# Value products in concurrent 64x64 and 32-row tiles of the TensorE array, with V loaded by head halves in rows of 64

## The chip, the cores and the metric

The kernel runs on one core of one Trainium2 chip. The metric is the device time of one execution in microseconds (us). Each kernel was run several times, in rounds that alternate with the kernel before on the same chip. Every comparison below is between fast runs. Only one timed run of any kernel here was slow, and it is left out.

## The reference, cut to what matters

```python
# q, k, v: (8 batches, 8 heads, 576 positions, 64), float32
k_p = k.reshape(B, H, 72, 8, 64).mean(axis=3)        # keys pooled by 8: 72 a head
v_p = v.reshape(B, H, 72, 8, 64).mean(axis=3)        # values pooled by 8
scores = matmul(q, k_p.T) / sqrt(64)
attn = exp(scores - max); attn = attn / sum(attn)
x = (attn @ v_p), heads side by side                 # (8 * 576 tokens, 512)
out = gelu(x @ w_in) @ w_out                         # 512 -> 2048 -> 512
```

## The kernel before

Attention of one batch is woven into the two big products of the batch before it ("hidden", L296, and "output", L301). Seven batches of 512 positions are handled this way in a steady rhythm. Batch 0 stands in the start, and the last 64 positions of every batch form a "rest" batch. The parts that the change touches:

```python
    def rows(t, b):                                   # pooled rows: 72 a head, 576 a batch, each of 8 x 64 numbers
        return t[b].rearrange("h (sp pl) d -> (h sp) pl d", pl=8)

    def load_half(b, which, eng):                     # 64 rows of k and 64 of v share one block of 128 partitions
        if which == "v":
            eng.dma_start(out=st[b]["kv"][64:128, 4], in_=rows(v, b)[0:64])
        else:
            eng.dma_start(out=st[b]["kv"][0:64, 4], in_=rows(k, b)[512:576])

    def load_main(b, which, c0, c1, eng):             # the other 512 rows, on 128 partitions
        t, w0, b0 = (k, 0, 0) if which == "k" else (v, 64, 5)
        src = rows(t, b)[w0 + 128 * c0:w0 + 128 * c1].rearrange("(c p) pl d -> p c pl d", p=128)
        eng.dma_start(out=st[b]["kv"][:, b0 + c0:b0 + c1], in_=src)
    ...
    def values(g, half, eng):                         # "value step": pooled v (masked, zero-padded) times e
            ...
                for x, (c, n) in enumerate(PARTS[pr]):
                    nc.tensor.matmul(out=xo[:, i, :], lhsT=vbd[:, g, n, :], rhs=eT[:, :, c, :],
                                     start=(x == 0), stop=(x == 1))
    ...
    def load_kv(n):                                   # all on one queue, in this order
            ...
            load_main(b, "k", 0, 4, nc.sync)
            load_half(b, "k", nc.sync)
            load_half(b, "v", nc.sync)
            load_main(b, "v", 0, 4, nc.sync)
    ...
                at(hooks, t0, pool, b, 0, 5)          # hooks: position among the matmuls of a batch
                at(hooks, t0, k_transpose_dma, b)     # kvb -> kTd, a DMA on the same queue as the loads
                at(hooks, t0 + 20, pool, b, 5, 9)     # v is pooled later than k
                at(hooks, 56, k_spread, b, ...)       # kTd -> kbd; the scores (from hook 67) wait for it
                ...
            at(hooks, 91, load_kv, n2)
```

In the views, DVE pools `kv` into `kvb`, `kTd<-kvb` is the DMA transpose of the pooled k, and `kbd` is its copy that the scores `sc` multiply. `eb` holds the normalised exponentials, `eT<-eb` are their DMA transposes, `xo` is the result of the value step, and `xT` is its copy for the hidden layer. Line numbers differ from kernel to kernel, so follow the tile names.

The softmax here doesn't subtract the row's maximum and nothing guards it: scores larger than these inputs give would overflow.

## Time and profile before

| | kernel before |
|---|---|
| time, median | 301.14 us (300.99 to 301.49, 4 runs) |
| span of the profiled run, granted TensorE clock | 299.3 us, 1.00 |
| first value step of the steady rhythm | 52.14 us |
| from one steady value step to the next | 30.35 us |
| value step, start of the last matmul before to the start of the first after | 1.94 us |
| k landed, v landed, kTd landed after a value step (batch at 142.77) | 6.9, 10.9, 14.6 us |
| scores begin after a value step | 17.70 us |

In the view of DMA issues each line gives tile, queue, kind, count, size, and the median time from issue to landing. These lines are of the kernel before:

```profile
kv<-in_v_dram SPq DMA_DIRECT2D x7, 1024.0 KB, 9.9
...
eT<-eb SPq DMA_TRANSPOSE x32, 2.6
...
kTd<-kvb SPq DMA_TRANSPOSE x6, 3.6
```

The lines that carry the bound (busy shares, chain) stand in the prediction. kTd lands 14.6 to 16.3 us after a value step, and the scores that need it start at 17.70. So PE's slack there is only 1.4 to 3.1 us, and the two copies into kbd take 0.5 to 1.1 us of it. And kTd is issued at 10.8 to 12.8 us, in the same queue as v, when v has just landed or is still on its way.

### The profile page before, as it was taken

The page shows a single profiled execution, that of the slowest core. Times are in us where ns is not written, and L with a number is a line of the kernel's source. Part 1 is how long each engine was busy: PE and PEld are TensorE (multiplying, and loading weights), DVE is VectorE, ACT ScalarE, POOL GpSimd, SP SyncE. Part 2 cuts the span into 40 slices and gives each one's busy share as a digit, 9 for nine tenths or more (in the row PEclk, how much of TensorE's full clock was granted, in tenths as well). Part 3 has the DMA queues.
Part 4 walks back from the last instruction along what each step waited for, and adds up shares of the span by engine and source line. Part 5 has one row for each costly group of instructions (what it writes and reads, how often), then busy time and mean ns, then how long its engine had stood idle before and what let it go on. Part 6 is the DMA issues. An engine that isn't in the chain of part 4 may idle for free.

```text
span 299.3 us, 4581 instructions
## 1 busy us (share of the span) xinstructions
PE 290.7 (97%) x1734; PEld 151.6 (51%) x1734; DVE 146.7 (49%) x241; ACT 158.2 (53%) x242; POOL 55.5 (19%) x71
## 2 busy tenths in 40 slices
PE   7869999999999999999999999999999999999996
PEld 7748844445444544454445444544444544444444
DVE  6895769164706570648073807381639100920012
ACT  1477783667157715672477246724773267426500
POOL 3252033230400240024012400240024000100000
PEclk9999999999999999999999999999999999999999
DMA  7999997995699459947993599049944800351012
GB/s 235 357 387 338 384 350 132 343 279 158 135 279 250 145 127 271 269 146 126 261 297 134 119 249 301 4 107 249 276 147 101 164 36 2 79 114 37 0 70 70
DMA packets 73221, 56.32 MB, mean 188 GB/s; under 512 B 45808, under 2 KB 55408, under 8 KB 73200
## 3 DMA queue, kind: packets, MB, share of 16 engines
q1 hardware_dynamic: 73056, 55.98, 68.2%
q8 instruction: 13, 0.21, 0.3%
q10 hardware_dynamic: 144, 0.07, 0.1%
q14 instruction: 8, 0.07, 0.1%
HBM read 36.70 MB, written 9.44 MB: 154 GB/s over the span
## 4 chain that ended last, share of the span: by engine, by line
PE 91%; DMA 3%; DVE 2%; SPq 1%; POOL 1%; issue 0%; POOLq 0%
PE mm L296 41%; PE mm L301 41%; PE xo L266 4%; DMA q_sb<-in_q_dram 3%; PE sc L208 2%; PE mm L329 1%; POOL eb L231 1%; SPq L98 1%; PE xo L272 1%; PE tp L193 1%; PE sc L213 0%; DVE w_in_b L80 0%; PE tp L240 0%; DVE w_out_b L80 0%; POOL q_b L80 0%; PE xo L255 0%
## 5 line engine op out<-in xcount | busy, mean ns | idle before, releaser
L301 PE MATMUL mm<-w_out_b,gT 128*128 128x512 bf16 x560 | 128.6, 379 | 0.5 <-DVE w_out_b L80 0.5
L296 PE MATMUL mm<-xT,w_in_b 128*128 128x512 bf16 (+1 forms) x640 | 127.6, 358 | 0.5 <-DVE xT L80 0.5
L298 ACT ACTIVATE gT<-mm 128x512 bf16<-128x512 f32 (+1 forms) x160 | 88.4, 555 | 47.0 <-PE mm L296 45.9
L296 PEld LDWEIGHTS <-w_in_b 128*128 128x128 bf16 x640 | 62.2, 98 | 62.6 <-issue 0.5
L301 PEld LDWEIGHTS <-gT 128*128 128x128 bf16 x560 | 53.4, 98 | 59.7 <-DVE w_out_b L80 0.7
L80 DVE COPY osb<-mm 128x512 f32<-128x512 f32 (+2 forms) x37 | 24.3, 658 | 62.9 <-PE mm L301 60.8
L78 ACT CAST xT<-xo 128x1024 bf16<-128x1024 f32 (+1 forms) x18 | 16.6, 966 | 56.8 <-PE xo L266 49.1
L228 DVE TENSOR_REDUCE den<-e 128x8 f32<-128x576 f32 x36 | 26.5, 736 | 38.0 <-ACT e L221 37.9
L148 POOL TENSOR_TENSOR vbd<-kvb,vmask 128x256 bf16<-128x256 bf16 (+2 forms) x40 | 21.2, 553 | 113.5 <-DVE kvb L130 113.4
L128 DVE TENSOR_TENSOR kv<-kv 128x1024 f32<-128x1024 f32 (+3 forms) x20 | 22.4, 1118 | 29.7 <-DMA kv<-in_v_dram 27.7
L231 DVE TENSOR_TENSOR eb<-e,r 128x576 bf16<-128x576 f32 x28 | 27.2, 970 | 1.0
L221 ACT ACTIVATE e<-sc 128x576 f32<-128x576 f32 x36 | 22.5, 650 | 9.6 <-ACT e L221 4.0
L231 POOL TENSOR_TENSOR eb<-e,r 128x576 bf16<-128x576 f32 x8 | 10.1, 1266 | 71.5 <-ACT e L221 41.1
L80 POOL CAST q_b<-q_sb 128x2048 bf16<-128x2048 f32 (+1 forms) x7 | 15.0, 2147 | 4.1 <-DMA q_sb<-in_q_dram 4.1
L208 PEld LDWEIGHTS <-qT 128*128 128x128 bf16 x128 | 10.1, 98 | 7.0 <-ACT qT L78 0.6
L208 PE MATMUL sc<-kbd,qT 128*128 128x144 bf16 x128 | 13.2, 226 | 0.2 <-ACT qT L78 0.2
L266 PE MATMUL xo<-eT,vbd 128*128 128x512 bf16 x56 | 13.2, 379 | 0.0
L129 DVE TENSOR_TENSOR kv<-kv 128x512 f32<-128x512 f32 (+3 forms) x20 | 12.8, 640 | 0.7
L410 PE MATMUL warm<-identb 128*128 128x128 bf16 x112 | 9.1, 249 | 1.4 <-POOL vmask L398 1.4
L494 ACT ACT_TABLE_LOAD x8 | 10.3, 1283 | 0.1
L80 DVE COPY kbd<-kTd 64x288 bf16<-64x288 bf16 x12 | 5.6, 467 | 8.3 <-DMA kTd<-kvb 8.2
L314 ACT ACT_TABLE_LOAD x7 | 9.0, 1283 | 0.1
(55 smaller groups left out, 99.5 us busy)
## 6 DMA issues: line engine op xcount, KB each, us to landing
out_dram<-osb SPq DMA_DIRECT2D x31, 256.0 KB, 6.7
kv<-in_k_dram SPq DMA_DIRECT2D x7, 1024.0 KB, 6.5
q_sb<-in_q_dram SPq DMA_DIRECT2D x7, 1024.0 KB, 5.9
kv<-in_v_dram SPq DMA_DIRECT2D x7, 1024.0 KB, 9.9
w_in_s<-in_moe_w_in_dram SPq DMA_DIRECT2D x4, 1024.0 KB, 13.0
w_out_s<-in_moe_w_out_dram SPq DMA_DIRECT2D x4, 1024.0 KB, 13.8
out_dram<-osb SPq DMA_DIRECT2D x9, 128.0 KB, 2.3
kv<-in_k_dram SPq DMA_DIRECT2D x2, 512.0 KB, 3.9
```

Of the source, the lines that this page charges most:

```text
L78: eng.copy(out=out, in_=in_)
L80: eng.tensor_copy(out=out, in_=in_)
L128: add(out=t[:, :, 0:4, :], in0=t[:, :, 0:4, :], in1=t[:, :, 4:8, :], op=ALU.add)
L148: eng.tensor_tensor(out=vbd[p0:128, b, n0:n1, :].rearrange("p (c r) (hh d) -> p c (r hh) d", c=max(m, 1), d=D), in0=kvb[p0:128, 4 + c0:4 + ...
L208: nc.tensor.matmul(out=o, lhsT=qT[:, j, pr, :], rhs=kbd[:, g, pr].rearrange("d hh s -> d (hh s)"), start=True, stop=True)
L221: nc.scalar.activation(out=e.rearrange("p (x h) s -> p x (h s)", x=2), in_=sc[:, :, 0:4 * Sp], func=ACT.Exp, scale=1.0 / 64.0)
L228: nc.vector.reduce_sum(out=den, in_=e, axis=AX.X)
L231: eng.tensor_tensor(out=eb[:, j, 128 * 5 - W:].rearrange("p (h s) -> p h s", s=Sp), in0=e, in1=r.unsqueeze(2).to_broadcast([128, H, Sp]), ...
L266: nc.tensor.matmul(out=xo[:, i, :], lhsT=vbd[:, g, n, :], rhs=eT[:, :, c, :], start=(x == 0), stop=(x == 1))
L296: nc.tensor.matmul(out=hp[:, 0:c1 - c0], lhsT=w_in_b[:, ko, fo * 128:(fo + 1) * 128], rhs=st[g]["xT"][:, ko, c0:c1], start=(ko == 0), stop ...
L298: nc.scalar.activation(out=gT[:, fo, c0:c1], in_=hp[:, 0:c1 - c0], func=ACT.Gelu_apprx_tanh)
L301: nc.tensor.matmul(out=o, lhsT=gT[:, fo, r * 128:(r + 1) * 128], rhs=w_out_b[:, fo, :], start=(fo == 0), stop=(fo == FO - 1))
```

## The change

The value product used 128x128 weights padded with zeros, because a head's 72 pooled rows don't fill whole partitions. The change stores v so that 64 rows of a head fill 64 neighbouring partitions. Heads 0 to 3 lie in the lower half, heads 4 to 7 in the upper. The remaining 8 rows of every head are gathered in one extra block. Two kinds of small tiles then multiply at once, and no multiplication spreads v into padded form. The softmax output is written in the same order, and so the normalisation is split in two instructions and the k copies in four.

```diff
     def load_half(b, which, eng):
+        dst = st[b]["kv"][:, 4].rearrange("(m i) pl d -> i m (pl d)", i=2)
         if which == "v":
-            eng.dma_start(out=st[b]["kv"][64:128, 4], in_=rows(v, b)[0:64])
+            src = v[b].rearrange("h (sp pl) d -> h sp (pl d)", pl=8)[:, 64:72]
+            eng.dma_start(out=dst[0], in_=src)
     def load_main(b, which, c0, c1, eng):
...
+            for x in range(2):
+                src = v[b].rearrange("h (sp pl) d -> sp h (pl d)", pl=8)[0:64, 4 * x + c0:4 * x + c1]
+                eng.dma_start(out=st[b]["kv"][64 * x:64 * x + 64, 5 + c0:5 + c1].rearrange("p c pl d -> p c (pl d)"),
+                              in_=src)
...
+    def values_rem(g, pr, o, blocks, cols):
+        p0 = 32 * pr
+        nc.tensor.matmul(out=o, lhsT=vrem[p0:p0 + 32, g].rearrange("p hh d -> p (hh d)"),
+                         rhs=st_eT[0][p0:p0 + 32, blocks, 4, cols], start=True, stop=False)
+    def values_main(g, h, o, blocks, cols):
+        r0, c0 = 64 * (h // 4), 64 * (h % 2)
+        nc.tensor.matmul(out=o[c0:c0 + 64], lhsT=vb[r0:r0 + 64, g, h % 4, :],
+                         rhs=st_eT[0][r0:r0 + 64, blocks, h % 4, cols], start=False, stop=True)
...
-        eng.tensor_tensor(out=eb[:, j, 128 * 5 - W:]..., in0=e, in1=r..., op=ALU.mult)
+        eng.tensor_tensor(out=eb[:, j, 0:64 * H]..., in0=e[:, :, 0:64], in1=r..., op=ALU.mult)
+        eng.tensor_tensor(out=eb[:, j, 64 * H:]..., in0=e[:, :, 64:Sp]..., in1=r..., op=ALU.mult)
...
-    load_half(0, "k", nc.sync)
-    load_half(0, "v", nc.sync)
+    load_half(0, "k", nc.scalar)
+    load_half(0, "v", nc.scalar)
```

## The prediction

> **What bounds the kernel now.** I read the page's busy shares first, then the chain that ended last, then the chain in order of time, and last the timeline of one batch. Busy shares and the chain's summary:
>
> ```profile
> PE 290.7 (97%) x1734; PEld 151.6 (51%) x1734; DVE 146.7 (49%) x241; ACT 158.2 (53%) x242; POOL 55.5 (19%) x71
> ...
> PE 91%; DMA 3%; DVE 2%; SPq 1%; POOL 1%; issue 0%; POOLq 0%
> ```
>
> PE is busy all the time and is also 91% of the chain, while every other engine is half idle. Matmuls overlap in the pipeline, so I trust the chain more than the busy sum. One batch of it, in order of time (start, length, what):
>
> ```profile
> 173.28 1.73 PE xo L266 x8
> 175.01 1.51 PE mm L301 x7
> 176.52 13.81 PE mm L296 x64
> 190.33 0.65 PE mm L301 x3
> 190.98 0.25 PE sc L208 x4
> ```
>
> 64 matmuls of 512 columns take 13.81 us, 216 ns each. From one value step to the next (173.28 to 203.64) it is 30.36 us: 136 such matmuls are 29.36 and 16 score matmuls at 62 ns are 1.0, so PE has no gap at all. A 512-column matmul removed from this stretch is worth 216 ns; work on another engine is worth nothing until it makes PE wait. The first 26 us are different: they are loads, pooling and softmax in turn, and the chain goes through DMA, POOL and DVE there (9.81 us of it is the second load of q).
>
> The value step is 8 matmuls of 512 columns, 1.73 us, in seven batches (L266); 64 matmuls of 64 columns, 1.87 us, for the rest batch (L272); 16 of 256 columns for batch 0 (L255). In all about 16 us of 299.
>
> **What the skill says.** The Trainium skill, "TensorEngine Tiling (Array Packing)", Key Properties, says that different tiles can load and multiply in parallel, and that changing the tiling mode drains the engine. This kernel already has one tiled step, the rest batch's scores in 128x64 tiles, so both claims can be read off the trace:
>
> ```profile
> 220.69 0.65 PE mm L301 x3
> 221.33 0.37 PE sc L213 x8
> 221.71 0.54 PE mm L301 x2
> ```
>
> Two L301 matmuls without a tiled step before them take 0.43, here 0.54. So the eight half-width matmuls cost 0.37 + 0.11 = 0.48 us. One after the other they would be 8 x 62 = 0.50, in pairs 0.25. The trace agrees with the page on both points: two column tiles do run at once (each pair starts 3 to 4 ns apart, next pair 62 ns on), and going in and out costs 0.23 us together, 0.115 per switch. For row tiles, "TensorE: Matmul & The Clock Gate", Part 3 (packing small matmuls), gives a measured 3.07x for four 32-row tiles of 512 columns; no row tile runs in this kernel, so that I take on the page's word. "PSUM", Bank collisions, says that two row tiles must not write one bank at once; the order of heads 0 1 4 5, then 2 3 6 7, puts the two row halves in different banks, so nothing has to be serialised for it.
>
> **The change, part by part.**
>
> *Values, seven batches.* Removed: 8 x 216 = 1.73 us. Added: four 32-row matmuls in one pack (216 + 3 x 4 = 228 ns), eight 64x64 matmuls in two packs of four (2 x 228 = 456), three switches, into 32-row, into 64x64 and back (3 x 115 = 345). Sum 1.03 us. Saved 0.70 us a batch, 4.9 us in seven. Twelve smaller weight loads in place of eight stay hidden under a 228 ns pack.
>
> *Values, rest batch.* Here the modes alternate for each of 8 batches: 16 switches. One round is a switch (95 of drain), a pack of four 64-column matmuls (27 + 12), a drain again (95), a pack (39) and a second pack that has to wait for its weights: in L213 the second pair started 84 ns after the first, 22 late, because of them; for 64-column matmuls I take 84. Sum about 350 ns, times 8 = 2.8 us in place of 1.87: 0.9 us lost.
>
> *Values, batch 0.* 8 x 109 = 0.87 us a half becomes 3 x 121 + 3 x 115 = 0.71. Only the second half is in the PE-bound part: 0.15 saved.
>
> *Evictions.* Two ACT casts in a row (1014 ns each) become one on ACT and one on DVE at once, now with the factor 0.125. DVE's copy of 512 PSUM columns took 687 ns, so 1024 take about 1.2 us. Seven L301 matmuls (1.51 us) lie after the value step, and the halves that the second pack finishes are asked for third and fourth by the reordered hidden layer, 0.43 us later. Hidden.
>
> *POOL.* The 40 spread multiplications (21.2 us busy) become eight small ones. POOL is 19% busy: nothing gained directly.
>
> *Normalisation.* Each softmax multiplication of 576 columns becomes one of 512 and one of 64. This is the part that I think will be paid for. The timeline of one batch:
>
> ```profile
> 166.84 1.01 DVE L231 TENSOR_TENSOR eb<-e,r 128x576 bf16<-128x576 f32 x1
> 167.18 2.42 POOL L80 CAST q_b<-q_sb 128x2048 bf16<-128x2048 f32 x1
> 167.27 4.18 SPq L244 DMA_TRANSPOSE eT<-eb  x3
> 167.78 0.74 DVE L228 TENSOR_REDUCE den<-e 128x8 f32<-128x576 f32 x1
> 168.62 0.20 DVE L230 RECIPROCAL r<-den 128x8 f32<-128x8 f32 x1
> 168.86 1.36 DVE L231 TENSOR_TENSOR eb<-e,r 128x576 bf16<-128x576 f32 x1
> ...
> 172.94 0.49 PEld L266 LDWEIGHTS <-vbd 128*128 128x128 bf16 x3 [0.16 <-issue]
> 173.12 0.59 PE L266 MATMUL xo<-eT,vbd 128*128 128x512 bf16 x2
> ```
>
> DVE works without a break up to 170.22, the last transpose goes out at 170.24, lands 2.6 us later (172.84, the view of DMAs gives 2.6 as the median), and the first value matmul starts at 173.12. The slack is 0.28 us; in the other steady batches it is 0.25 to 0.31, in the rest batch and the last one 0.6, in batch 1 1.6. DVE needs 760 ns for 576 columns alone; at 1.04 ns a column that is 161 fixed, so 512 + 64 columns are 693 + 228, less about 83 that independent DVE instructions overlap: +0.08 us. Three of the four are on DVE, two of them run beside POOL and are stretched by a third to four fifths: together +0.3 to +0.4. That is the slack and 0.1 more: five batches x 0.1 = 0.5 us lost.
>
> *Spreading k.* Two copies become four, on DVE in the steady state, some 0.35 us more. In batch 2 the scores start only 0.2 us after the copies: 0.2 lost in total.
>
> *Loads.* The same bytes in 64-partition transfers. "DMA: Bandwidth & Descriptors", the descriptor swizzle, pairs engines with partition halves, and the same page calls the SBUF ports the bottleneck, so 64 neighbouring partitions have half of the ports. The trace agrees in part: at 5.0 to 6.0 us, when the two 64-partition loads run, 258 to 286 GB/s move, against 385 to 415 around them. At 270 GB/s one MB of v takes 3.9 us and not 2.7. In the steady state v has time. At the start the second load of q queues behind v and is on the chain: up to 1 us later. Two more copies of k on ACT, and both evictions of batch 0 now behind the fourth score block, are on that path too; against it stands POOL, which no longer slows DVE (a multiplication at 15.06 took 1.29 us beside it, 0.82 alone). Net 0.8 us lost, give or take 0.8.
>
> Sum: -4.9 + 0.9 - 0.15 + 0.5 + 0.2 + 0.8 = -2.65. From 301.11 that is 298.5 us.
>
> **Rivals.**
> 1. *Full gain:* the value step falls to about 1 us and nothing is given back, and the start gets quicker because POOL is free: -4.9 - 0.15 + 0.9, less up to 1.5 at the start, 295.5. For it: DVE and POOL lose work. Against it: the 0.28 us of slack, and the rest batch's 16 switches.
> 2. *A new wait eats it:* the last transpose lands 0.5 us late in the five tight batches, because the small strided multiplication costs more than its columns. 5 x 0.5 in place of the 0.5 above makes 300.5. For it: DVE has no gap there. Against it: most of the extra fits in the slack.
> 3. *Row tiles do not run at once:* then only column pairs overlap and the step is 4 x 216 + 4 x 216 + 0.35, 2.07 us, 0.35 more than now: 298.5 + 4.9 + 2.4 = 305.8. Against it the page's 3.07x.
> 4. *The v load delays the pool of v, the copies of k and the scores:* two batches have a v that landed late already (95.0, 125.1) with some 0.6 us left before the scores; a microsecond more costs 0.4 each. About 299.3.
>
> **Range and chances.** The middle is 298.5. The start (0.8 either way), the stall per batch (0 to 0.4, times five) and the switch (0.08 to 0.15, 21 of them in the seven batches and 16 in the rest batch) give about 2.5 us either way: 296.0 to 301.0. Two per cent is 6.0 us, more than rival 1 gives even with the start going well, so faster by over 2% gets 0.07; slower by over 2% needs rival 3 and more, 0.02; the rest is within 2%.
>
> **What would show it.** Value matmuls in packs of four with starts 3 to 5 ns apart; 1.0 us from the first of them to the next L301 matmul, where now 1.73; 2.5 to 3 us for the rest batch; a PE gap of about 0.1 us before the value step, put down to the eT transpose; POOL at 12% or so; first hidden matmul after 19.26 us. I am wrong if the packs are serial, if a switch costs much more than 0.115 us, if the gap before the value step is over 0.3 us, or if the start moves by more than 1.6 us.

## The result

| | before | after |
|---|---|---|
| time, median (4 fast runs each) | 301.14 us | 308.27 us (307.33 to 309.31) |
| ratio, 95% interval | | 1.0236 (1.0201 to 1.0271) |
| span, granted clock | 299.3 us, 1.00 | 306.8 us, 0.993 |

A ratio is always the mean time of one kernel's fast runs over the mean of the other's fast runs of the same rounds, so not quite the ratio of the medians quoted beside it. The result is correct, and the kernel is 2.4% slower. The prediction of 298.5 us was wrong, and so were its range and its class.

The page of the kernel after has busy shares, the granted clock in 40 slices (tenths) and the chain that ended last:

```profile
PE 286.3 (93%) x1775; PEld 147.6 (48%) x1802; DVE 157.1 (51%) x291; ACT 151.5 (49%) x238; POOL 38.7 (13%) x46
...
PEclk9979999999999999999999999999999999999999
...
PE 38%; DMA 17%; DVE 12%; SPq 6%; issue 3%; ACT 1%; DVEq 0%; ACTq 0%
```

PE was 91% of the chain, and is now 38%. DMA and DVE have come into it. The clock falls to 7 tenths once, in the third slice. The waits of PE, before and after (us in total, times, longest), give the place. Before, the only one at the scores was this:

```profile
PE sc L208 <- ACT qT L78: 0.2, 1, 0.2
```

After:

```profile
PE sc L207 <- DVE kbd L85: 7.5, 5, 2.4
PE vp L148 <- DMA kv<-in_v_dram: 2.0, 1, 2.0
```

Five times, once in each steady batch, the scores wait for `kbd`. And once, in the start, the pooling of v on PE (`vp`) waits for v itself. Neither wait was there before. The chain in order of time, for one steady batch (its value step is at 118.31; start, length, what), shows what is behind `kbd`. Its first line is the small v load, which shares a block with the last rows of k, so that the pooling of k waits for it:

```profile
120.37 6.03 DMA kv<-in_v_dram
...
129.72 6.30 DMA kTd<-kvb
...
136.28 0.24 DVE kbd L85
...
136.66 0.41 PE sc L207 x4
```

The transpose of k is issued 11.4 us after the value step, as before, but takes 6.3 us. The view of DMA issues of the kernel after shows what stands in front of it:

```profile
kv<-in_v_dram SPq DMA_DIRECT2D x14, 512.0 KB, 8.1
...
eT<-eb SPq DMA_TRANSPOSE x32, 2.6
...
kTd<-kvb SPq DMA_TRANSPOSE x6, 4.8
```

The 4.8 us for kTd is misleading: where an 8-engine load shares a semaphore, the view can't tell the landings, and of these six it could tell one. In the chain the four other steady transposes take 5.99, 6.30, 6.52 and 5.93 us, against a median of 3.6 before. v is now two transfers of 512 KB in place of one of 1 MB, and in the trace each takes about 2.5 us, one after the other (landed at 10.8 and 13.2 us after this value step). That is 210 GB/s. Before, the whole MB landed 2.9 us after the small load ahead of it in the batch at 142.77. That is 363 GB/s, and over six batches it was 2.6 to 3.7 us, once 5.2. Now it is 4.3 to 5.3. So v is done 12.8 to 13.4 us after a value step (mean 13.1), where it was 9.8 to 13.0 before (mean 11.5). The transpose stands behind it. That is not all of it: in the kernel before, kTd landed 3.3 to 3.7 us (2.7 in the first batch) after the later of its own issue and v's landing, and here it lands 4.4 to 4.8 us after v's in the four batches that wait behind v. Why it is longer stays open.

The arithmetic did what it was meant to do. In the timeline of one value step of the kernel after:

```profile
149.41 0.39 PE L253 MATMUL xo<-eT,vrem 32*128 32x512 bf16 x4
149.73 0.63 PE L258 MATMUL xo<-eT,vb 64*64 64x512 bf16 x8
150.29 1.04 PE L331 MATMUL mm<-w_out_b,gT 128*128 128x512 bf16 x4
```

Twelve matmuls run in three packs of four. The starts within a pack are 3 to 4 ns apart. From the start of the last matmul before to the start of the first after it is 1.20 us, where it was 1.94. The rest batch's step went from 2.08 to 2.92 us (as a_oldloads below shows it; the kernel after has 3.14, with one matmul record missing).

To place the loss I cut each span in three at the value steps: the start up to the first steady value step, the five periods from it to the sixth, and the tail.

| us | start | five periods | tail | span |
|---|---|---|---|---|
| before | 52.14 | 151.33 | 95.83 | 299.3 |
| after | 55.63 | 155.96 | 95.21 | 306.8 |
| difference | +3.49 | +4.63 | -0.62 | +7.5 |

In the tail only one more batch is loaded, and no score waits for it (its kTd lands 15.8 us after the value step, the scores start at 16.96). There the change wins what its matmuls save: two short steps at -0.75 each and the rest batch at +0.83 make -0.67. The same saving must also be in the five periods (5 x -0.75 = -3.7), so some 8.4 us were lost there.

### The profile page after: what moved, and what is told of

Read it like the earlier page. It is cut to its first block, busy times and chain, and to the rows that moved or that the text cites. A ratio compares the mean times of both kernels' runs of the same rounds, so it can differ in the third digit from the quotient of the medians.

```text
span 306.8 us, 4712 instructions
## 1 busy us (share of the span) xinstructions
PE 286.3 (93%) x1775; PEld 147.6 (48%) x1802; DVE 157.1 (51%) x291; ACT 151.5 (49%) x238; POOL 38.7 (13%) x46
## 4 chain that ended last, share of the span: by engine, by line
PE 38%; DMA 17%; DVE 12%; SPq 6%; issue 3%; ACT 1%; DVEq 0%; ACTq 0%
PE mm L331 20%; PE mm L326 13%; DMA kTd<-kvb 9%; DMA kv<-in_v_dram 6%; SPq L198 3%; DVE den L227 3%; DMA kv<-in_k_dram 2%; DVE kv L140 2%; PE sc L207 2%; DVE osb L85 2%; SPq L105 1%; PE mm L359 1%; DVE eb L230 1%; DVE kv L141 1%; SPq L246 1%
## 5 line engine op out<-in xcount | busy, mean ns | idle before, releaser
L331 PE MATMUL mm<-w_out_b,gT 128*128 128x512 bf16 x543 | 126.6, 379 | 1.6 <-DVE w_out_b L85 0.5
L140 DVE TENSOR_TENSOR kv<-kv 128x1024 f32<-128x1024 f32 (+3 forms) x19 | 21.7, 1140 | 45.7 <-DMA kv<-in_v_dram 39.3
L85 DVE COPY osb<-mm 128x512 f32<-128x512 f32 (+2 forms) x37 | 24.3, 659 | 35.4 <-PE mm L331 31.3
L268 ACT ACTIVATE xT<-xo 128x1024 bf16<-128x1024 f32 (+1 forms) x12 | 9.5, 812 | 55.7 <-PE xo L258 55.7
L220 ACT ACTIVATE e<-sc 128x576 f32<-128x576 f32 x36 | 23.0, 651 | 17.3 <-PE sc L207 11.4
L230 DVE TENSOR_TENSOR eb<-e,r 128x512 bf16<-128x512 f32 x28 | 24.1, 860 | 1.0
L230 POOL TENSOR_TENSOR eb<-e,r 128x512 bf16<-128x512 f32 x8 | 9.2, 1144 | 105.7 <-ACT e L220 72.1
L207 PE MATMUL sc<-kbd,qT 128*128 128x144 bf16 x128 | 13.2, 226 | 8.4 <-DVE kbd L85 7.5
L270 DVE TENSOR_SCALAR xT<-xo 128x1024 bf16<-128x1024 f32 (+1 forms) x12 | 11.3, 956 | 17.3 <-PE xo L258 17.2
L207 PEld LDWEIGHTS <-qT 128*128 128x128 bf16 x128 | 9.6, 97 | 16.3 <-issue 10.1
L85 POOL CAST q_b<-q_sb 128x2048 bf16<-128x2048 f32 (+1 forms) x7 | 12.4, 1768 | 24.2 <-DMA q_sb<-in_q_dram 24.2
L156 POOL TENSOR_TENSOR vrem<-kvb,vmask 128x128 bf16<-128x128 bf16 x8 | 3.4, 428 | 93.3 <-DVE kvb L142 87.3
L440 PEld LDWEIGHTS <-identb 128*128 128x128 bf16 x112 | 8.8, 120 | 1.5 <-POOL vsel L428 1.4
L85 DVE COPY kbd<-kTd 64x288 bf16<-64x288 bf16 (+3 forms) x24 | 3.8, 201 | 11.3 <-DMA kTd<-kvb 11.2
```

The lines of the kernel that those rows point to most:

```text
L85: eng.tensor_copy(out=out, in_=in_)
L140: add(out=t[:, :, 0:4, :], in0=t[:, :, 0:4, :], in1=t[:, :, 4:8, :], op=ALU.add)
L207: nc.tensor.matmul(out=o, lhsT=qT[:, j, pr, :], rhs=kbd[:, g, pr], start=True, stop=True)
L220: nc.scalar.activation(out=e.rearrange("p (x h) s -> p x (h s)", x=2), in_=sc[:, :, 0:4 * Sp], func=ACT.Exp, scale=1.0 / 64.0)
L230: eng.tensor_tensor(out=eb[:, j, 0:64 * H].rearrange("p (h s) -> p h s", s=64), in0=e[:, :, 0:64], in1=r.unsqueeze(2).to_broadcast([128, H ...
L270: eng.tensor_scalar(out=out, in0=in_, scalar1=0.125, scalar2=None, op0=ALU.mult)
```

## The experiments

My theory P was this: the form of the load costs the time. Each half of v fills 64 neighbouring partitions, moves at 210 GB/s, and holds up the transpose of k that stands behind it. The Trainium skill has this in "SBUF — State Buffer", Door 1: The DMA port swizzle: what counts is how many of 16 ports the partitions reach, 64 neighbouring ones reach 8, and its table gives 196 GB/s for 1 MiB there against 328 for 128 partitions. This agrees within 12%: 210 and 363. The rivals were: the new normalisation and k copies on DVE (the arithmetic's own costs), and the small v load. That load reads 8 heads of 8 rows, and the trace shows 8 engine completions for it where the others have 16. The skill, "DMA: Bandwidth & Descriptors", Why a DMA increments its semaphore by 16 and not by 1, says that the number of engines is the largest that divides the slowest dimension of both sides. That is 8 here, and the trace agrees.

The same three-part cut for all runs (profiled run, us); labels are explained below. Times are medians of 4 fast runs, in hybrid2 of 5 and in the three below it of 6. The three parts come from a single execution, and where the start waits, the executions differ: those of a_v2q took 302.26 to 305.56 us, and the profiled ones of a_v2q and a_half16 are the fastest of their four. So differences of 2 or 3 us between the starts of such kernels should not be read:

| label | start | five periods | tail | time | ratio to before (95%) |
|---|---|---|---|---|---|
| a_oldloads | 52.23 | 148.46 | 95.21 | 297.49 | 0.988 (0.987 to 0.989) |
| b_v64 | 53.72 | 153.67 | 95.91 | 305.39 | 1.014 (1.013 to 1.016) |
| b_half8 | 52.77 | 151.33 | 95.80 | 301.95 | 1.002 (1.000 to 1.004) |
| b_both | 59.52 | 153.27 | 95.91 | 309.82 | 1.030 (1.026 to 1.034) |
| a_half16 | 55.66 | 150.25 | 95.19 | 303.98 | 1.009 (1.006 to 1.012) |
| a_vlate | 56.97 | 166.04 | 100.09 | 325.05 | 1.079 (1.076 to 1.081) |
| a_v2q | 56.92 | 148.38 | 95.20 | 304.21 | 1.010 (1.005 to 1.015) |
| a_v2qs | 58.34 | 149.08 | 96.18 | 305.00 | 1.012 (1.009 to 1.014) |
| a_v2qs_rg | 58.95 | 151.17 | 94.38 | 304.43 | 1.012 (1.008 to 1.016) |
| best1 | 58.87 | 149.01 | 94.42 | 304.45 | 1.010 (1.007 to 1.012) |
| best1_h16 | 60.39 | 149.72 | 94.39 | 304.21 | 1.010 (1.006 to 1.014) |
| best3 | 58.38 | 149.20 | 94.42 | 302.74 | 1.003 (1.000 to 1.006) |
| best4 | 60.41 | 149.95 | 94.44 | 305.65 | 1.013 (1.008 to 1.018) |
| hybrid | 53.20 | 151.18 | 94.32 | 300.41 | 0.996 (0.994 to 0.999) |
| hybrid2 | 53.34 | 153.49 | 94.37 | 303.40 | 1.009 (1.007 to 1.012) |
| hybrid3 | 53.23 | 154.07 | 94.40 | 303.34 | 1.006 (1.004 to 1.008) |
| hybrid3b | 53.32 | 157.58 | 94.50 | 307.46 | 1.022 (1.019 to 1.025) |
| hybrid4 | 53.29 | 153.25 | 94.46 | 302.71 | 1.002 (0.999 to 1.005) |

### a_oldloads: all of the new arithmetic, the loads of before

The rows of v are then in the wrong places, so the result is wrong.

```diff
-            src = v[b].rearrange("h (sp pl) d -> h sp (pl d)", pl=8)[:, 64:72]
-            eng.dma_start(out=dst[0], in_=src)
+            eng.dma_start(out=st[b]["kv"][64:128, 4], in_=rows(v, b)[0:64])
...
-            for x in range(2):        # two halves of 64 partitions
+        src = rows(t, b)[w0 + 128 * c0:w0 + 128 * c1].rearrange("(c p) pl d -> p c pl d", p=128)
+        eng.dma_start(out=st[b]["kv"][:, b0 + c0:b0 + c1], in_=src)
```

> The changed kernel with all its new arithmetic, but v and the two small blocks loaded exactly as the kernel before loads them (128 partitions in one transfer, the small ones contiguous, all on SP's queue). The rows land in the wrong places, so the result is wrong on purpose; every instruction on the engines and every wait is as in the changed kernel. Theory L (the loads alone lose the time; the arithmetic gains what was predicted): a period of 29.6 to 29.7 us between value steps against 30.36, no PE wait before the scores, the first hidden matmul within 0.8 us of 19.26; 297.0 us (295.5 to 298.5). Rival D (split normalisation, more copies of k, switches of tiling mode cost more than they save): over 300.5.

It took 297.49 us. The chain on its page is PE's again:

```profile
PE 87%; DMA 8%; SPq 2%; DVE 1%; issue 0%; POOL 0%; DVEq 0%
```

Against the kernel after, the start is 3.40 us shorter, the five periods 7.50, the tail the same. Together they are the whole difference of the spans, 10.9 us. So the whole loss comes from how v and the small blocks are loaded, and the rest of the change taken together gains. (In a_oldloads the small k block has its old place too, and batch 0's small loads are back on SP's queue. No run takes these two apart from the loads of v.) The gain of 3.56 us is the prediction's sum for the arithmetic: -4.9 + 0.9 - 0.15 + 0.5 = -3.65. Its stall before the value step is there too. The five periods should be 3.7 us shorter than before and are 2.87. The missing 0.85 us lies just before the value steps: there the distance from the last matmul to the step is 0.09 to 0.31 us longer than the 0.31 us that it is without a wait (0.8 us over the five). I put this down to the new normalisation; no run tests that alone.

### b_v64: the kernel before, each v load cut into two halves of 64 partitions

```diff
+        if which == "v":
+            for x in range(2):
+                p_ = slice(64 * x, 64 * x + 64)
+                eng.dma_start(out=st[b]["kv"][p_, b0 + c0:b0 + c1], in_=src[p_])
```

> The kernel before, with nothing changed but each v load split into two transfers of 64 partitions on the same queue. Theory P: v takes about 5 us after the half v, not 3.1; the k transposes land some 2.4 us later and PE waits before the scores in the batches with little slack (up to 2 us each), and the start is 2 us later: 304 us (302.5 to 306.5). Rivals K and D: 301, as before.

It took 305.39 us, 4.2 over the kernel before and inside the expected range, with the same rows in the same places and nothing else changed. The view of DMA issues and the waits of PE:

```profile
kv<-in_v_dram SPq DMA_DIRECT2D x14, 512.0 KB, 9.7
...
kTd<-kvb SPq DMA_TRANSPOSE x6, 5.1
```

```profile
PE sc L213 <- DVE kbd L80: 1.6, 3, 0.7
```

kTd went from 3.6 to 5.1 us, and the same wait appears, though smaller. By the table 2.3 us of the loss lie in the five periods and 1.6 in the start, where PE now waits 1.3 us for v itself. In the kernel after it is larger because its value step is 0.75 us shorter: without a wait the scores would start 16.87 us after the value step and not 17.70 (a_oldloads shows it). So the saving itself takes 0.83 us from the time that k has. This shows that the halves alone cost time, and by this path.

### a_vlate: the kernel after, v loaded behind the transpose of k and pooled later

```diff
-            load_main(b, "v", 0, 4, nc.sync)          # in load_kv
-                at(hooks, t0 + 20, pool, b, 5, 9)
+                at(hooks, t0, load_main, b, "v", 0, 4, nc.sync)   # behind the k transpose
+                at(hooks, 57, pool, b, 5, 9)
```

> The changed kernel, but in the steady batches the two v loads are issued behind the k transpose and v is pooled after the copies of k; the loads themselves and the start stay as they are. Theory P: the k transpose lands about 3 us after its issue again, the waits before the scores go, the late start stays: 300.5 us (299 to 302.5). Rival K: 306 to 308, since the small v load still stands before the pooling of k. Rival D: 308.

It took 325.05 us, a clear miss. The waits before the scores were gone, but another was far larger:

```profile
PE xo L253 <- DMA eT<-eb: 13.6, 7, 3.9
```

v now lands some 7 us after its issue. DVE waits for it, 51.9 us in 12 waits, and the softmax is issued behind that pooling. "Late" was wrong for v too: v must be pooled before the softmax of the next batch begins.

### a_half16: the kernel after, the small v load contiguous again, on 16 engines

```diff
-            src = v[b].rearrange("h (sp pl) d -> h sp (pl d)", pl=8)[:, 64:72]
+            src = rows(v, b)[0:64].rearrange("m pl d -> m (pl d)")
```

> The changed kernel, but the small v load reads 64 rows that follow one another (the wrong ones, so a wrong result on purpose), which spreads it over 16 engines instead of 8. Theory P: at most 0.5 us less, 307.8 us (307 to 308.5). Rival K: most of the loss goes, 301 to 303.

It took 303.98 us (wrong rows), 4 us less than the kernel after. I had expected next to nothing, so theory P alone fell short. The periods shrink by 5.7 us, the start not at all. (The profiled execution is the fastest of its four; the medians differ by 4.3 us.) In the view of the waits:

```profile
PE sc L207 <- DVE kbd L85: 1.9, 4, 0.7
```

The waits at the scores drop from 7.5 to 1.9 us, though v lands no earlier than in the kernel after (12.5 to 13.4 us). In the four batches that wait kTd lands 16.7 to 17.1 us after the value step, and in the kernel after 17.3 to 18.05. What is measured is this difference of 0.5 to 0.9 us; how a load on 8 engines brings it about stays open. In the first steady period the wait of 2.4 us is gone altogether: there k's load was issued 3.4 us before the value step, and in the kernel after only 0.8.

### b_half8 and b_both: the kernel before with the 8-engine load, alone and with the halves

```diff
-            eng.dma_start(out=st[b]["kv"][64:128, 4], in_=rows(v, b)[0:64])
+            src = v[b].rearrange("h (sp pl) d -> h sp (pl d)", pl=8)[:, 64:72]
+            eng.dma_start(out=st[b]["kv"][64:128, 4].rearrange("p pl d -> p (pl d)"), in_=src)
```

> The kernel before, and only the small v load as 8 heads of 8 rows, on 8 engines (wrong rows: wrong result on purpose). If the two forms of load add: both together were 8.7 us more than before and the halves alone 4.2, so 305.6 us (304.5 to 306.5). If the 8 engines cost only beside halves in turn: 301 to 302.

> The kernel before with both new forms of load and none of the new arithmetic: each v load in two transfers of 64 partitions, and the small v load as 8 heads of 8 rows, which runs on 8 engines (it reads wrong rows: wrong result on purpose). Theory L: more than the 4.2 us of the split alone, since every later transfer on those 8 engines comes about 1.4 us later: 308.5 us (306.5 to 311). If the 8 engines matter only beside the new arithmetic: 305.4, as with the split alone.

Alone, the 8-engine load costs 0.7 us (301.95). Together with the halves of b_v64 the cost is 8.8 us (309.82), and the two alone would sum to 4.9. Both results are wrong. The table of three parts shows where they fail to add: the periods of b_both are no longer than those of b_v64, but its start is 7.4 us longer than before, where the two alone have 1.6 and 0.6. Waits and windows of b_both (window, its length, busy PE, PEld, DVE, ACT, POOL, then the clock, the DMA share and GB/s):

```profile
PE vp L142 <- DMA kv<-in_v_dram: 4.3, 1, 4.3
```

```profile
12.00:15.00 3.00, 0.78 (x8) 0.44 (x8) 2.17 (x5) 1.49 (x3) 0.65 (x2) 1.00 1.15 184
15.00:17.00 2.00, 0.00 (x0) 0.00 (x1) 1.93 (x4) 0.00 (x0) 0.53 (x1) 0.76 1.10 326
17.00:20.00 3.00, 2.97 (x14) 3.00 (x15) 0.80 (x2) 0.00 (x0) 1.04 (x1) 0.50 1.06 386
```

PE waits 4.3 us for v, and when v is there the granted clock is half. A late v in the start thus costs twice. The kernel after shows the same: it waits 2.0 us, and between 14 and 20 us its clock is 0.64 to 0.79. Why the two loads together make v so late stays open. The transfers move among those of w_in and q, and no run here separates them.

### a_v2q, a_v2qs and a_v2qs_rg: the second half of v on ACT's queue

```diff
+                q_ = nc.scalar if x else eng          # a_v2q; "if x and b" in a_v2qs
-                eng.dma_start(out=st[b]["kv"][64 * x:64 * x + 64, ...
+                q_.dma_start(out=st[b]["kv"][64 * x:64 * x + 64, ...
```

> The changed kernel, but the second 64-partition half of every v load is issued on ACT's queue, so that both halves move at once. Theory P (two neighbouring-partition halves in one queue move in turn, each at some 210 GB/s, and the k transposes behind them land late): both halves land within 3.2 us of the half v instead of 5, PE's waits before the scores fall from 8.3 us in total to under 2, the first hidden matmul comes 1 to 2 us earlier; 299 us (297.5 to 301). Rival K (the small v load on 8 engines delays the pooling of k): 306 or more. Rival D (more and smaller DVE instructions: the copies of k, the split normalisation): 308.

> The changed kernel, correct, with the second v half on ACT's queue in all batches but the first, whose loads stay as they are. Theory L: the steady part as with both halves on two queues throughout (243.6 us from the first steady value step to the end in that trace), the start as in the changed kernel: 301.0 us (299.5 to 302.5). Rival D: 304 or more.

> As the one before it, and in the rest batch every second batch adds its 32-row matmuls after the 64x64 ones, so that the tiling mode changes 8 times and not 16. If a switch drains some 95 ns: the rest batch's value step falls from 2.6-2.8 us to about 1.9-2.0 and the time by 0.75 us, 300.3. If the switches are not what costs there: no change.

a_v2q is correct and took 304.21 us, where 299 was expected. Its periods are those of a_oldloads (148.38 and 148.46): the whole steady loss is gone. The view of DMA issues shows how:

```profile
kv<-in_v_dram ACTq DMA_DIRECT2D x7, 512.0 KB, 5.7
...
eT<-eb SPq DMA_TRANSPOSE x32, 3.4
...
kTd<-kvb SPq DMA_TRANSPOSE x6, 2.9
```

It isn't that the halves move at once. On SP's queue the loads stand behind the e transposes, which wait for the softmax. ACT has nothing in the way and issues its half some 11 us earlier, so only one half is left in front of kTd (2.9 us, from the four landings of six that the view can tell). The price is in the middle line: the e transposes that it passes rise from 2.6 to 3.4 us. They still land in time here, just.

The start remained the problem (56.92). a_v2qs kept the first batch on one queue, expecting 301 us, and took 305.00. ACT's half of batch 1 now passed that batch's own k and q and w_out (k landed at 33.0 us, in the kernel after at 31.3; w_in was not late). The chain ends the start with 5.74 us of an e transpose, for which the first steady value step waits 1.4 us, and the start became 58.34. a_v2qs_rg also let the rest batch alternate the order of its two tile kinds, 8 mode switches in place of 16. Its step fell from 2.92 to 2.09 us as expected, and the tail from 96.18 to 94.38, but the start took it back.

### best1, best1_h16, best3 and best4: other places for v in the start

```diff
+    load_main(0, "v", 0, 2, nc.sync, (0,))            # best1: first batch's second half later, from ACT's queue,
+    nc.vector.memset(st[0]["kv"][64:128, 5:9, 0, 0:1], 0.0)   # held back by this memset
+    load_main(0, "v", 0, 2, nc.sync, (1,))
...
-    load_main(1, "v", 0, 4, nc.sync)
+    at(hooks, 76, load_main, 1, "v", 0, 4, nc.sync)   # best1 and best3: batch 1's v from within the matmuls
+                q_ = nc.scalar if x and b > 1 else eng   # best4: ACT's queue from the third batch on
```

> A correct version meant to win: the changed kernel with the two v halves on two queues in every batch (in the first batch ACT's is held back by a one-column memset on DVE until about 5.8 us, in the second it is issued late from the hidden layer, so that neither runs ahead of q and the weights), the small loads of the first batch back on SP behind k, and the rest batch with 8 changes of mode. If the turn-taking halves were the larger part of the loss: first hidden matmul within 1.5 us of 19.3, no wait before the scores; 299.0 us (297.5 to 301.0). If the small load on 8 engines holds everything behind it: 302 to 304.

> As best1, but the small v load reads 64 rows that follow one another, over 16 engines (wrong result on purpose): the cost of the 8 engines by itself, with the halves already on two queues. If they cost what the skew of some 1.4 us between first and last engine suggests: 1.5 us less than best1, 297.5 (296 to 299). If they cost only beside halves that move in turn: the same as best1.

> As best1, but the first batch's two halves stay on SP's queue in turn. They take some 5 us for 1 MB and not 2.7, and PE waits for them at 12 us: 1 to 2.5 us slower than best1, 301.0 (299.5 to 303).

> The changed kernel, correct, with the second v half on ACT's queue from the third batch on only, so that nothing overtakes the weights in the start, and the rest batch with 8 changes of mode. Start as in the changed kernel (first steady value step at 55.6 us), steady part 243.4 us as in best1: a span of 299.1, 300.7 us (299.5 to 302).

They took 304.45, 304.21, 302.74 and 305.65 us. best1 and best4 missed. best3 fell inside its range, but it was meant to be slower than best1 and was faster. The periods are near the best (149.0 to 150.0) and the rest batch is short, but the start is 58.4 to 60.4 us. In best1 the half on ACT's queue moves beside q and w_in, and the chain in order of time is 11 us of q's load:

```profile
5.07 11.08 DMA q_sb<-in_q_dram
...
16.20 1.05 POOL q_b L85
...
17.99 1.19 PE vp L151 x4
```

best1_h16 is best1 with the contiguous small load (wrong), and its time is the same within 1 us: once only one half stands in front of kTd, no cost of the 8 engines can be seen. In best4 the start is lost at its very end, in one wait before the first steady value step:

```profile
PE xo L254 <- DMA eT<-eb: 4.6, 1, 4.6
```

ACT's half of batch 2 was issued at 50.81 and landed at 59.60, and the e transposes issued around it landed at 59.88 and 60.28. So not every loss in the start comes from its own bytes: this one is the meeting of ACT's half with the e transposes that hybrid and hybrid4 below turn on.

### hybrid: the loads of before in the first two batches, sorted by PE

```diff
+        if b < 2:                                     # load as the kernel before does, pool into kvb,
+            src = rows(v, b)[64 + 128 * c0:64 + 128 * c1].rearrange("(c p) pl d -> p c pl d", p=128)
+    def permute_v(b, eng, tag):                       # then bring the pooled rows to their places
+        for h in range(H):
+            ...
+                nc.tensor.matmul(out=ps[64 * x:64 * x + 64, h % 4, :], lhsT=band[:, o:o + 64], rhs=kvb[:, 4 + i, 0, :], ...)
```

> As best4, correct, and the first two batches load v as the kernel before does; their pooled v is brought into the new layout on PE by 16 small matmuls with shifted identities. If the rest of the loss is the start's loads: first steady value step at 53 to 53.5 us (52.2 in the kernel with the old loads, and up to 1 for the permutation), steady part 243.4; 298.2 us (296.8 to 299.8). If the start is lost to something else: 300.7 as best4.

This is correct and took 300.41 us (299.63 to 300.89), ratio 0.9963 (0.9935 to 0.9990): faster than both kernels, by 0.4% over the kernel before, though it missed the expected 298.2. The start is down to 53.20 us, the clock is 1.0, and the tail is the short one. (Here ACT's half of batch 2 was issued at 43.75, clear of the e transposes, so this start is not a clean test of the first two batches' loads.) Its periods are 2.8 us over those of a_v2q. PE waits before the value step, and the e transposes have risen:

```profile
PE xo L290 <- DMA eT<-eb: 2.4, 3, 1.1
```

```profile
eT<-eb SPq DMA_TRANSPOSE x32, 3.9
...
kTd<-kvb SPq DMA_TRANSPOSE x6, 2.7
```

The first e transpose of a batch was issued at 133.98 and landed 7.0 us later, since ACT's half of v was on its way at that time. Why it cost more here than in a_v2q, which issues it at the same place, isn't settled.

### hybrid2, hybrid3, hybrid3b and hybrid4: where the second half may stand

The four differ from hybrid only in when ACT issues its half: right after the value step, 8 and 16 hidden matmuls into the next batch, and a third of a batch earlier.

```diff
-            load_main(b, "v", 0, 4, nc.sync)                                     # hybrid: both halves at 91
+                at(hooks, 122, load_main, ..., "v", 0, 4, nc.sync, (1,))         # hybrid2
+                at(hooks, 8, load_main, b, "v", 0, 4, nc.sync, (1,))             # hybrid3; at 16: hybrid3b
+                at(hooks, 50, load_main, b2, "v", 0, 4, nc.sync, (1,))           # hybrid4
```

> As hybrid (first two batches load v as the kernel before does and sort it on PE, two queues for the halves of v from the third batch on, rest batch with modes alternating eight times), but the half of v on ACT's queue is issued just after the value step and no longer some 6 us before the other loads, so that it moves nothing while the e transposes run. Theory P (what is left of the loss in hybrid is the transfers of v disturbing the e transposes ahead of the value step): the waits of 0.65 to 1.3 us before the value step go, some 2 to 3 us in all, no wait before the scores comes back, and the time is 298.0 us (296.8 to 299.5), 1% under the kernel before. Rival Q (the waits come from the normalisation's split multiplications or from the transposes themselves): waits stay, 300.4 as hybrid. Rival R (v issued this late lands too late and DVE's pooling of it blocks what comes after): waits before the scores or the value step come back at over 1 us a batch, 302 or more.

> As hybrid2, with the half of v on ACT's queue issued some 4.5 us after the value step (eight hidden matmuls into the next batch) instead of right after it. hybrid2 showed the waits for the e transposes gone (the longest before a value step 0.42 us) but k landing at 9 to 9.8 us after the value step and not at 6 to 7.8, because the half of v shared the engines with it. Theory P (the two halves of v have to move after k, and at the same time as one another): k lands at 6 to 7.5 us, v at 10.5 to 11.5, no wait of over 0.3 us before the scores or the value step in the steady state, 298.0 us (296.8 to 299.5). Rival R (any split of v over two queues disturbs k or the transposes): waits of over 0.5 us a batch stay, 301 or more.

> As hybrid3, the half issued another eight matmuls (1.7 us) later. Theory P: k as in hybrid3, v at 12 to 12.5 us, the transpose of k waits behind less of it, DVE's pooling of v begins later by about a microsecond; waits of 0 to 0.5 us, 298 to 299.5 us. Rival R: as there, 301 or more.

> As hybrid, with the half of v on ACT's queue issued a third of a batch earlier (at the 50th hidden matmul, some 7 us ahead of the first e transpose), so that it has landed before the e transposes begin and lies before the load of k too. hybrid put it among the e transposes (they landed late, waits of 0.65 to 1.3 us before the value step), hybrid2 and hybrid3 put it beside k and behind q (waits of 0.4 to 1.8 us before the scores). Theory P (only the place matters): the e transposes land 2.6 us after their issue, k at 6 to 7.8 us and v at 10 to 10.7 us after the value step as in hybrid, no wait of over 0.35 us in the steady state, 297.6 us (296.6 to 299.0). Rival R (any place costs something): the issue on ACT's queue holds up the activations of the hidden layer, or q lands late and the cast of q with it; waits of over 0.5 us a batch, 300.5 or more.

All four missed their ranges, the first three each in its own way. In hybrid2 (303.40 us) the e transposes land in 2.6 us again, but k lands at 8.9 to 9.8 us after the value step (11.5 once) where hybrid had 5.7 to 7.8: the half moved beside k and took its time from it, as though the two went one after the other. In hybrid3 and hybrid3b (303.34 and 307.46) k was undisturbed, but the half landed at 14.4 to 16.3 us, at kTd's time. All three have the wait at the scores again, 4.7 to 6.8 us in four waits. This rejects hybrid2's theory that only the e transposes were in the way, and keeps the part of it that they were.

In hybrid4 the half moves before the e transposes, where SP's queue has only q. The view of DMA issues and the waits of PE:

```profile
eT<-eb SPq DMA_TRANSPOSE x32, 2.6
...
kTd<-kvb SPq DMA_TRANSPOSE x6, 3.7
```

```profile
PE sc L244 <- DVE kbd L87: 2.7, 1, 2.7
```

Three periods in a row are 29.67, 29.67 and 29.74 us, against 30.35 before (the next is 30.38, with a wait of 0.7 us for the e transposes). That is nearly all of the 0.75 that the value step saves, with no loss left for the loads. But the first period is 33.79 us: batch 2's k transpose (issued at 65.71) met the half of batch 3 there (issued at 65.96, landed at 71.74) and landed at 71.98, PE waited 2.7 us, and then ran at a granted clock of 0.53 for 3.6 us. So the whole took 302.71 us. The place is right for the rhythm and wrong for its first turn. From the parts, hybrid4 with a first period of 29.7 would take some 298.6 us (302.71 less 4.1). That is an estimate from the profiled execution and the median, and no run shows it.

## Why the prediction was wrong

- **What bounds the kernel** was right for the kernel before, and a_oldloads is PE-bound as foreseen. "Work on another engine is worth nothing until it makes PE wait" is what happened, on the DMA queue.
- **Values, seven batches.** Right: predicted 0.70 us saved a batch, measured 0.75. The packs of four ran at once, and each change of tile kind cost 93 to 99 ns over the plain start distance of 216, against the 115 that I took from the pairs of L213.
- **Values, rest batch and batch 0.** Right: predicted +0.9 and -0.15, measured +0.83 and -0.21.
- **Spreading k.** Wrong in direction, with little weight: the copies were put at 0.35 us more, and the four take 0.64 to 0.67 us in all, where the two took 0.5 to 1.1.
- **Normalisation.** Right in kind: a stall before the value step, put at 0.5 us in all. a_oldloads has 0.85 there, from whatever cause. In the kernel after it is hidden behind the larger wait.
- **Loads.** This is the step that failed: "In the steady state v has time." The sum had +0.2 us for the k copies and the scores and +0.8 for the start. Measured: the kernel after takes 10.8 us more than a_oldloads (308.27 and 297.49), in the profiled runs 7.5 in five periods and 3.4 in the start. Four things went into it.
  1. The rate. The prediction took 270 GB/s from a stretch in which two small loads ran among others. The contrast that it read was not clean either: 258 to 286 GB/s then, and 385 to 402 from 8.5 to 10.5 us, but only 272 to 332 between 6 and 8 us. One half by itself shows 210. The two halves take 4.3 to 5.3 us, not 3.9.
  2. What stands behind v. Only v's own users were looked at. The transpose of k is issued in the same queue some 11 us after the value step, and v is still moving then. b_v64 shows the halves alone: 4.2 us, of which 2.3 in the five periods come this way.
  3. The deadline. The saving brings the scores 0.83 us closer to the load. Much of this could be worked out from the prediction's own trace: kTd at 14.6 to 16.3 us, and its own 1.2 us more for v (3.9 less 2.7), is 15.8 to 17.5, with the scores due at 16.87 and the copies still to come. With the 5.2 us that the halves take (less 2.9 to 3.6) it is 16.2 to 18.6.
  4. The 8-engine load was not seen at all (4 us between the kernel after and a_half16), nor that a wait of PE in the start costs clock.
- **Rival 4** had the mechanism, "the v load delays the pool of v, the copies of k and the scores", but sized it at 0.8 us in two batches. It was in all five. The prediction's own sign of being wrong, a start that moves by more than 1.6 us, came true as well (3.49).
- **The range** had no term for the loads in the periods, so no combination of its errors could reach 308.

That the loads cause the loss, and where, is shown by a_oldloads, b_v64 and a_half16. What stays open: why the two load forms together cost 8.8 us and not 4.9 in the kernel before, how the 8-engine load delays the k transpose, and how the 3.4 us of the start divide among the halves, the 8-engine load and the small loads' move to ACT's queue.

## What to carry to other kernels

When a change alters a transfer, look beyond who waits for it, and list everything that is issued behind it in the same queue, with the slack of each from the trace. When the change also shortens a step, take its saving off that slack first. Then test the arithmetic and the data movement apart, with a wrong result if need be: one run (a_oldloads) told more here than all attempts to repair the start.

## What the Trainium skill lacked or had wrong

- "SBUF — State Buffer", Door 1: its rate for 64 neighbouring partitions holds here (210 GB/s for 512 KB against its 196 for 1 MiB). Its advice is about the transfer itself. What no page gives is the cost to a DMA transpose that stands behind such a load in the queue: kTd's median went from 3.6 to 5.1 us in b_v64.
- "DMA: Bandwidth & Descriptors", Issuing engines are not separate DMA queues: it says that a second issuing engine only saves issue time. In hybrid2 k and half of v did share the engines as it says. But it lacks that a second queue lets a load pass what the first is waiting for, which was worth 7.6 us of the five periods in a_v2q (155.96 to 148.38), and cost the e transposes 0.8 us each in the median.
- "DMA: Bandwidth & Descriptors", Why a DMA increments its semaphore by 16 and not by 1: the rule for the number of engines holds (8 for 8 heads). It lacks what an 8-engine load costs those behind it: 4 us in the kernel after, 0.7 us in the kernel before, no cost that could be seen within 1 us in best1.
- "TensorEngine Tiling (Array Packing)", Key Properties: it says that a mode switch drains the array but gives no cost. Here it was 93 to 99 ns a switch.
- "TensorE: Matmul & The Clock Gate", Part 1, gives an idle window of some 3.4 us before the clock falls. Here the clock fell after shorter waits: 2.0 us in the start of the kernel after (0.79, then 0.64) and 2.7 us in hybrid4 (0.53 for 3.6 us), while one of 2.4 us in the kernel after left it at 1.0.
